# Top-32 attention and a gated feed-forward on one core: the sums of a softmax are spread before their reciprocal is taken

## The chip, the cores and the metric

The kernel runs on 1 core of a Trainium2 chip. The metric is the device time of one execution in microseconds (us); less is better. Before the change it is 1622.12 us, the median of 3 runs (1620.75 to 1624.53).

## The reference

```
scores = scale * q @ k.T                        # 8 batches, 8 heads, 576 positions, head size 64
kth    = the 32nd largest score of each row
scores = where(scores >= kth, scores, -1e9)
attn   = exp(scores - max(scores))
attn   = attn / (sum(attn) + 1e-9)
x      = (attn @ v), heads side by side         # 4608 tokens x 512
gate   = 1 / (1 + exp(-(x @ w_gate)))           # d_ff 1536
out    = (gate * (x @ w_val)) @ w_out           # all in float32
```

## The kernel before, in words

The attention goes tile by tile: a tile is 128 queries of two heads (a pair), or, where 576 leaves a rest of 64 queries, 64 of each head in one tile (then J is 1, else 2). For a tile TensorE makes the scores (`scores`, L203 and L219), ScalarE brings them to SBUF, VectorE searches the largest ones (`select`: MAX8 and MATCH_REPLACE8, L284 to L290), ScalarE and GpSimd mark and keep the scores under a bound (L296, L302, L303), VectorE finds the 32nd largest (L310), and ScalarE takes the exponentials e (L233). `masked` then zeroes in e what is under the 32nd largest and has VectorE accumulate the row's sum in the same instruction (L238). What follows in `masked` is the place of the change: GpSimd adds 1e-9 to the [128, J] sums (L241), VectorE takes their reciprocals (L242), and GpSimd spreads each of them over 128/J columns of a [128, 128] tile `inv` (L244).

`turn` turns e by TensorE transposes (L321, L326), ScalarE reads them out of PSUM (L322). `weigh` is called for one or two tiles of a pair: it multiplies the turned e with the values into one PSUM bank (`po`, L340 to L348), turns `inv` by a transpose into another part of the same bank (`rb`, L351), has ScalarE read the turned reciprocals into SBUF (`rs`, L354), and VectorE multiplies the output out of PSUM with them (`xf`, L357; for the rest of 64 queries L361). ScalarE and GpSimd split xf into two parts of lower precision, xh and xl (L364, L365). The pool of that bank has one buffer: the next `weigh` waits until xf has been read. There are 160 tiles and 112 calls of `weigh`, 48 with 256 columns of reciprocals and 64 with 128.

Three tiles of 128 tokens of all four pairs make a unit of 384 tokens. For it `ffn` runs the feed-forward part: matmuls with split operands (L396 to L398 into `pz`, L415 to L417 into `po`), Tanh, multiply and split on ScalarE, VectorE and GpSimd (L401 to L404), output by DMA. `run` lays attention and feed-forward work beside each other. In the first stage of the program, before any unit is ready, the weights are split as well (`split_weight`, L130 to L150: DMA, ScalarE, VectorE, GpSimd, TensorE, ScalarE, DMA), and the keys of later batches (L169, L171).

The order of instructions on each engine is drawn by the framework's scheduler from the dependences and its own costs; each engine then works strictly in that order. Names in the rows below end in numbers of tiles: xf_2_3 is tile 2 of pair 3.

Of the kernel before, what the change touches and what calls it, by code (L numbers as in the profile page):

```python
# [10 lines left out]
F32 = mybir.dt.float32  # L11
# [4 lines left out]
AF = mybir.ActivationFunctionType  # L16
ALU = mybir.AluOpType
# [11 lines left out]
def tile_topk_attention_then_gated_ffn(  # L29
# [8 lines left out]
    nc = tc.nc  # L38
    P = 128
    B, H, _, S = k.shape  # L40
# [194 lines left out]
    def masked(J, s, kth, st, e, nm):  # L235

        for j in range(J):
            nc.vector.scalar_tensor_tensor(  # L238
                e[:, j], s[:, j], kth[j], e[:, j], op0=ALU.is_ge, op1=ALU.mult, accum_out=st[:, 4 + j : 5 + j]
            )  # L240
        nc.gpsimd.tensor_scalar(st[:, 4 : 4 + J], st[:, 4 : 4 + J], 1e-9, None, op0=ALU.add)  # L241
        nc.vector.reciprocal(st[:, 6 : 6 + J], st[:, 4 : 4 + J])  # L242
        inv = bi.tile([P, P], F32, tag="inv", name=f"inv_{nm}")
        nc.gpsimd.tensor_copy(  # L244
            inv.rearrange("p (j d) -> p j d", j=J), st[:, 6 : 6 + J].unsqueeze(2).to_broadcast([P, J, P // J])
        )
        return e, inv

# [82 lines left out]

    def weigh(et, vt, n, invs, pieces, nm):

# [15 lines left out]

        for t, inv in enumerate(invs):  # L350
            nc.tensor.transpose(rb[:, t * P : (t + 1) * P], inv, ident)  # L351
        rs = b2.tile([P, 2 * P], F32, tag="rs", name=f"rs_{nm}")
        m = len(invs) * P
        nc.scalar.activation(rs[:, :m], rb[:, :m], AF.Copy)  # L354
        xf = b2.tile([P, 2 * P], F32, tag="xf", name=f"xf_{nm}")[:, :n]
# [72 lines left out]
    def run(general):  # L428
# [32 lines left out]
        for n in range(len(steps) + 2):  # L461
# [35 lines left out]
            nm = f"{mark}{b}_{i}_{p}"  # L497
            e, inv = done.pop(n - 2)
            if i == first or (i - first) % 2 == 0 or i == NT:
                et, o, invs = b2.tile([P, 9, 2 * P], F32, tag="et", name=f"et_{nm}"), 0, []  # L500
            turn(e, i, et, o, nm)
            invs.append(inv)
            o += P if i < NT else REM
            if len(invs) == 2 or i >= end - 1 or i == NT - 1:

                t, left, pieces = b * S + (i + 1 - len(invs)) * P, o, []
                while left:
# [10 lines left out]
                    t, left = t + k, left - k  # L518
                weigh(et, values[g, p], o, invs, pieces, nm)
            at += (P if i < NT else REM) / NP  # L520
# [76 lines left out]
```

## Time and profile before

| | |
|---|---|
| median of 3 runs | 1622.12 us (1620.75 to 1624.53) |
| the profiled execution | 1619.79 us |
| its span, first to last instruction | 1618.0 us |
| mean granted TensorE clock | 0.981 of 2.4 GHz |

The profile is of one execution, so a sum made from its rows is a sum against 1619.79 us; its span leaves out 1.8 us around the program. A busy time is the time in which an engine had at least one instruction at work. The idle time of an engine is put down to the instruction that it waited for last.

### The profile page before, as it was taken

The numbers are of one execution on the slowest core, as the hardware profiler recorded it, in microseconds if no ns is written. First come the engines' busy times: TensorE is split into PE (matmuls) and PEld (weight loads), VectorE is DVE, ScalarE is ACT, GpSimd is POOL, SyncE is SP. The second block draws the span as 40 slices with busy tenths as digits, with TensorE's granted clock in tenths as the row PEclk, the third lists the DMA queues.
The fourth block names the chain that finished last, engine by engine and source line by source line (L and its number), as shares of the span: only waits on it lengthen the run. The fifth ranks groups of instructions, "written<-read, shape, count | busy, mean of one in ns | idle before, by whom it ended". The sixth has DMA issues, their size and how long they took to land.

```text
span 1618.0 us, 33444 instructions
## 1 busy us (share of the span) xinstructions
PE 1553.3 (96%) x10226; PEld 1391.1 (86%) x10226; DVE 1265.3 (78%) x5748; ACT 1168.9 (72%) x2615; POOL 1206.8 (75%) x1923
## 2 busy tenths in 40 slices
PE   5878999899999999999999999999999999999998
PEld 2434897789999999999999999989999999999998
DVE  5999878988888779887888778888788778888300
ACT  6888778977777777777777777777777777777322
POOL 3679977897767896787877886788876996776413
PEclk9878999999999999999999999999999999999999
DMA  7556745665655565565555665655565665554575
GB/s 240 191 187 223 262 166 190 208 217 207 220 191 187 197 247 198 207 227 204 200 193 189 222 234 188 218 175 206 202 200 181 217 225 197 187 200 165 194 268 178
DMA packets 88989, 331.98 MB, mean 205 GB/s; under 512 B 9952, under 2 KB 36576, under 8 KB 61920
## 3 DMA queue, kind: packets, MB, share of 16 engines
q1 hardware_dynamic: 88800, 329.75, 59.0%
q8 instruction: 83, 1.36, 0.3%
q14 instruction: 106, 0.87, 0.2%
HBM read 301.40 MB, written 28.31 MB: 204 GB/s over the span
## 4 chain that ended last, share of the span: by engine, by line
PE 75%; POOL 7%; DVE 4%; ACT 3%; issue 1%; DMA 1%; POOLq 0%; SPq 0%; ACTq 0%
PE pz L396 11%; PE pz L397 11%; PE pz L398 11%; PE pss L219 8%; PE pt L321 6%; PE po L340 6%; PE po L415 5%; PE po L417 5%; PE po L416 5%; POOL u L302 3%; PE po L342 2%; DVE e L238 1%; PE po L351 1%; POOL k L171 1%; DVE kths L310 1%
## 5 line engine op out<-in xcount | busy, mean ns | idle before, releaser
L302 POOL TENSOR_TENSOR u<-s,under 128x288 f32<-128x288 f32 x576 | 444.5, 794 | 83.3 <-ACT under L296 77.3
L284 DVE MAX8 cand<-s 128x8 f32<-128x72 f32 x2304 | 348.1, 218 | 73.4 <-ACT s L226 63.3
L396 PE MATMUL pz<-xh,w 128*128 128x384 f32 x1120 | 383.9, 344 | 0.5 <-ACT gf L401 0.5
L397 PE MATMUL pz<-xl,w 128*128 128x384 f32 x1120 | 380.1, 339 | 0.3 <-POOL xl L365 0.3
L398 PE MATMUL pz<-xh,w 128*128 128x384 f32 x1120 | 379.5, 339 | 0.0
L238 DVE SCALAR_TENSOR_TENSOR e<-s,kths,e 128x576 f32<-128x576 f32 x288 | 291.7, 1020 | 2.8 <-ACT e L233 2.7
L310 DVE MAX8 kths<-u 128x8 f32<-128x584 f32 x288 | 219.6, 763 | 88.5 <-POOL u L303 86.3
L296 ACT ACTIVATE under<-s,leads 128x576 bf16<-128x576 f32 x288 | 223.4, 777 | 43.1 <-DVE leads L288 38.1
L233 ACT ACTIVATE e<-s,st 128x576 f32<-128x576 f32 x288 | 210.1, 774 | 52.0 <-POOL st L292 51.3
L404 POOL TENSOR_TENSOR gl<-gf,gh 128x384 fp32r<-128x384 f32 x144 | 156.0, 1084 | 92.4 <-ACT gh L403 90.3
L322 ACT ACTIVATE et<-pt 128x384 f32<-128x384 f32 x384 | 179.8, 490 | 46.4 <-PE pt L321 45.8
L396 PEld LDWEIGHTS pz<-xh,w 128*128 128x128 f32 x1120 | 210.8, 188 | 1.7 <-ACT gf L401 1.0
L397 PEld LDWEIGHTS pz<-xl,w 128*128 128x128 f32 x1120 | 211.4, 189 | 1.0 <-POOL xl L365 0.6
L398 PEld LDWEIGHTS pz<-xh,w 128*128 128x128 f32 x1120 | 211.1, 189 | 0.0
L226 ACT ACTIVATE s<-pss 128x576 f32<-128x576 f32 x256 | 164.5, 643 | 42.1 <-PE pss L219 41.4
L416 PE MATMUL po<-gl,w 128*128 128x384 f32 x560 | 189.5, 340 | 0.4 <-POOL gl L404 0.3
L415 PE MATMUL po<-gh,w 128*128 128x384 f32 x560 | 188.8, 350 | 0.9 <-ACT acc L419 0.9
L321 PE MATMUL pt<-ident,e 128*128 128x128 f32 x1152 | 184.9, 279 | 4.9 <-DVE e L238 2.6
L417 PE MATMUL po<-gh,w 128*128 128x384 f32 x560 | 187.4, 338 | 0.0
L321 PEld LDWEIGHTS pt<-ident,e 128*128 128x128 f32 x1152 | 144.7, 143 | 28.9 <-DVE e L238 6.5
L219 PE MATMUL pss<-k,qh 128*128 128x288 f32 (+2 forms) x588 | 167.5, 303 | 2.0 <-ACT s L226 2.0
L219 PE MATMUL pss<-k,ql 128*128 128x288 f32 (+2 forms) x588 | 159.1, 293 | 0.0
(105 smaller groups left out, 3318.6 us busy)
## 6 DMA issues: line engine op xcount, KB each, us to landing
w<-ws SPq DMA_DIRECT2D x210, 1024.0 KB, 4.9
v<-in_v_dram SPq DMA_DIRECT2D x64, 352.0 KB, 3.3
wraw<-in_w_dram SPq DMA_DIRECT2D x36, 512.0 KB, 4.4
ws<-wsplit SPq DMA_DIRECT2D x36, 512.0 KB, 3.5
qraw<-in_q_dram SPq DMA_DIRECT2D x140, 128.0 KB, 3.0
kraw<-in_k_dram SPq DMA_DIRECT2D x56, 288.0 KB, 3.8
out_dram<-acc SPq DMA_DIRECT2D x48, 192.0 KB, 4.0
q<-in_q_dram SPq DMA_DIRECT2D x20, 128.0 KB, 3.5
```

The lines of the kernel that those rows point to most:

```text
L219: nc.tensor.matmul(ps[:, half, o : o + n], x[:K, h * P : (h + 1) * P], ks[h][:K, k0 : k0 + n], start=t == 0, stop=t == len(todo) - 1,)
L238: nc.vector.scalar_tensor_tensor(e[:, j], s[:, j], kth[j], e[:, j], op0=ALU.is_ge, op1=ALU.mult, accum_out=st[:, 4 + j : 5 + j])
L284: nc.vector.max(cand[:, j, 8 * g : 8 * g + 8], s[:, j, g * SEG : (g + 1) * SEG])
L302: nc.gpsimd.tensor_tensor(u[:, j, c], s[:, j, c], under[:, j, c], op=ALU.mult)
L310: nc.vector.max(kths[:, at[j] : at[j] + 8], u[:, j])
L321: nc.tensor.transpose(pt[:, c], ef[:, k0 : k0 + P], ident)
L396: nc.tensor.matmul(ps, wt[:, u, 0, d], xh, start=d == 0, stop=False)
L397: nc.tensor.matmul(ps, wt[:, u, 0, d], xl, start=False, stop=False)
L398: nc.tensor.matmul(ps, wt[:, u, 1, d], xh, start=False, stop=d == NP - 1)
L415: nc.tensor.matmul(ps, wt[:, e % 2, 0, f], gh, start=f == 0, stop=False)
L416: nc.tensor.matmul(ps, wt[:, e % 2, 0, f], gl, start=False, stop=False)
L417: nc.tensor.matmul(ps, wt[:, e % 2, 1, f], gh, start=False, stop=f == FG - 1)
```

## The change

In `masked` the sums go to GpSimd alone: one instruction reads the [128, J] sums as a broadcast, adds 1e-9 and writes the [128, 128] tile, now `wide`. The small reciprocal goes. `weigh` turns `wide` as it turned `inv`, and in place of ScalarE's copy VectorE takes the reciprocal of the turned sums while it reads them out of PSUM. The rest of the diff renames `inv` and `invs`.

```
-        nc.gpsimd.tensor_scalar(st[:, 4 : 4 + J], st[:, 4 : 4 + J], 1e-9, None, op0=ALU.add)
-        nc.vector.reciprocal(st[:, 6 : 6 + J], st[:, 4 : 4 + J])
-        inv = bi.tile([P, P], F32, tag="inv", name=f"inv_{nm}")
-        nc.gpsimd.tensor_copy(
-            inv.rearrange("p (j d) -> p j d", j=J), st[:, 6 : 6 + J].unsqueeze(2).to_broadcast([P, J, P // J])
-        )
-        return e, inv
+        wide = bi.tile([P, P], F32, tag="wide", name=f"wide_{nm}")
+        nc.gpsimd.tensor_scalar(
+            wide.rearrange("p (j d) -> p j d", j=J),
+            st[:, 4 : 4 + J].unsqueeze(2).to_broadcast([P, J, P // J]),
+            1e-9,
+            None,
+            op0=ALU.add,
+        )
+        return e, wide
...
-        for t, inv in enumerate(invs):
-            nc.tensor.transpose(rb[:, t * P : (t + 1) * P], inv, ident)
+        for t, wide in enumerate(wides):
+            nc.tensor.transpose(rb[:, t * P : (t + 1) * P], wide, ident)
         rs = b2.tile([P, 2 * P], F32, tag="rs", name=f"rs_{nm}")
-        m = len(invs) * P
-        nc.scalar.activation(rs[:, :m], rb[:, :m], AF.Copy)
+        m = len(wides) * P
+        nc.vector.reciprocal(rs[:, :m], rb[:, :m])
```

VectorE's order around the last multiply of the first unit, xf_2_3. Before (L242 is the small reciprocal, cand, tops and leads belong to the search, kths and e to L310 and L238, wraw and wt_lead to the split of a weight):

```order
L310 MAX kths<-u_4_0_1756 128x8
L290 MATCH_REPLACE cand_3_1_1831<-tops_3_1_1832,cand_3_1_1831 128x64
L288 MAX leads<-cand_3_1_1831 128x8
L284 MAX cand_4_1_1925<-s_4_1_1743 128x8 x8
L238 SCALAR_TENSOR_TENSOR e_4_0_1755,st_4_0_1753<-s_4_0_1567,kths,e_4_0_1755 128x576
L288 MAX leads<-cand_3_1_1831 128x8
L242 RECIPROCAL st_3_0_1657<-st_3_0_1657 128x2
L138 TENSOR_SCALAR wt_lead_0_2967<-wt_lead_0_2967 128x512
L288 MAX tops_4_1_1926<-cand_4_1_1925 128x8
L357 TENSOR_TENSOR xf_2_3_1814<-po_2_3_1801,rs_2_3_1812 128x128
L242 RECIPROCAL st_4_0_1753<-st_4_0_1753 128x1
```
Now (lines after the change in `masked` stand 2 higher, L356 is the reciprocal out of PSUM, L359 the multiply):

```order
L292 MATCH_REPLACE cand_3_1_1805<-tops_3_1_1806,cand_3_1_1805 128x64 x2
L286 MAX cand_4_1_1897<-s_4_1_1719 128x8 x8
L140 TENSOR_SCALAR wt_lead_1_1530<-wraw_1_1528 128x512
L290 MAX tops_3_1_1806<-cand_3_1_1805 128x8 x2
L356 RECIPROCAL rs_2_3_1786<-po_2_3_1775 128x128
L290 MAX tops_4_1_1898<-cand_4_1_1897 128x8
L292 MATCH_REPLACE cand_3_1_1805<-tops_3_1_1806,cand_3_1_1805 128x64 x2
L138 TENSOR_SCALAR wt_lead_0_2925<-wt_lead_0_2925 128x512
L359 TENSOR_TENSOR xf_2_3_1788<-po_2_3_1775,rs_2_3_1786 128x128
L292 MATCH_REPLACE cand_4_1_1897<-tops_4_1_1898,cand_4_1_1897 128x64
L290 MAX leads<-cand_3_1_1805 128x8
```
The multiply stands at nearly the same place. Its reciprocal rs_2_3 stands four rows in front of it, with searches and a step of a weight split between them, and the small reciprocals are gone from both sides.

TensorE's order where the feed-forward part begins (`pz` with xh and xl). Before (wrest belongs to the split of a weight, pss are scores, pt turned exponentials):

```order
L219 MATMUL pss_4_1_0_1744<-k_1_3_321,q_4_1_1565 128x64
L147 MATMUL wrest_0_1534<-wsplit_1530,minus 128x512
L148 MATMUL wrest_0_1534<-wsplit_1530,plus 128x512
L146 MATMUL wrest_1_1551<-wraw_1_1548,ident 128x512
L396 MATMUL pz_0_0_0_1963<-xh_0_614,w_0_1959 128x384
L397 MATMUL pz_0_0_0_1963<-xl_0_615,w_0_1959 128x384
L398 MATMUL pz_0_0_0_1963<-xh_0_614,w_0_1959 128x384
L396 MATMUL pz_0_0_0_1963<-xh_1_996,w_0_1959 128x384
L397 MATMUL pz_0_0_0_1963<-xl_1_997,w_0_1959 128x384
L398 MATMUL pz_0_0_0_1963<-xh_1_996,w_0_1959 128x384
L396 MATMUL pz_0_0_0_1963<-xh_2_1378,w_0_1959 128x384
L397 MATMUL pz_0_0_0_1963<-xl_2_1379,w_0_1959 128x384
```
Now (L342 to L344 are the weighing, L353 the transpose of `wide`, L398 to L400 the feed-forward):

```order
L342 MATMUL po_2_3_1775<-et_2_3_1759,v_3_1044 64x128
L343 MATMUL po_2_3_1775<-et_2_3_1759,v_3_1044 64x128
L344 MATMUL po_2_3_1775<-et_2_3_1759,v_3_1044 128x128
L353 MATMUL po_2_3_1775<-ident,wide_2_3_1680 128x128
L323 MATMUL pt_3_0_2_1863<-ident,e_3_0_1637 128x128 x3
L146 MATMUL wrest_1_1531<-wraw_1_1528,ident 128x512
L398 MATMUL pz_0_0_0_1933<-xh_0_608,w_0_1929 128x384
L399 MATMUL pz_0_0_0_1933<-xl_0_609,w_0_1929 128x384
L400 MATMUL pz_0_0_0_1933<-xh_0_608,w_0_1929 128x384
L398 MATMUL pz_0_0_0_1933<-xh_1_984,w_0_1929 128x384
L399 MATMUL pz_0_0_0_1933<-xl_1_985,w_0_1929 128x384
```
The first feed-forward matmuls stood behind the split's wrest_1 and in front of the turns of tile 3_0 and of the weighing po_2_3. Now they stand behind all turns of tile 3_0 and behind the weighing po_2_3 with its transpose.

## Rows read from the trace of the kernel before

**Rows 1.** The page's first part: busy time of each engine, its share of the span, and its instructions (PEld is TensorE's weight load, DVE VectorE, ACT ScalarE, POOL GpSimd).

```profile
PE 1553.3 (96%) x10226; PEld 1391.1 (86%) x10226; DVE 1265.3 (78%) x5748; ACT 1168.9 (72%) x2615; POOL 1206.8 (75%) x1923
```

**Rows 2.** Busy time by stage of the span. Columns: the stage in us and its length, then for each engine its busy us with the number of its instructions, then the granted TensorE clock as a share of 2.4 GHz, the busy share of the DMA engines, and GB/s.

```profile
0.00:160.00 160.00, 117.27 (x467) 60.07 (x467) 136.75 (x596) 127.88 (x258) 106.74 (x177) 0.84 0.64 210
160.00:360.00 200.00, 190.29 (x1231) 164.14 (x1230) 173.01 (x743) 159.65 (x356) 170.22 (x263) 0.99 0.61 212
360.00:1500.00 1140.00, 1134.49 (x7855) 1059.14 (x7854) 938.78 (x4373) 850.75 (x1935) 892.27 (x1442) 1.00 0.59 202
1500.00:1618.00 118.00, 111.21 (x680) 107.74 (x678) 16.79 (x40) 30.57 (x67) 37.54 (x43) 0.99 0.60 213
```

**Rows 3.** The waits of TensorE's matmuls from 360 to 1500 us, longest first: who waited for whom, us in total, times, longest.

```profile
PE pt L321 <- ACT et L322: 2.2, 1, 2.2
PE pss L219 <- ACT s L226: 1.8, 1, 1.8
```

**Rows 4.** TensorE's timeline where the feed-forward part begins: the first matmul of it and the ninth, with seven more between them. Columns: start, us, engine, line, operation, output and inputs, shapes.

```profile
161.23 0.76 PE L396 MATMUL pz<-xh,w 128*128 128x384 f32 x1
...
163.05 0.34 PE L398 MATMUL pz<-xh,w 128*128 128x384 f32 x1
```

**Rows 5.** Busy time by stretch, with the columns of rows 2: the first stage after the start-up, its last 40 us, and two stretches in which the splitting of weights goes on.

```profile
40.00:160.00 120.00, 96.11 (x408) 50.99 (x406) 113.85 (x480) 103.47 (x213) 92.24 (x140) 0.82 0.59 200
120.00:160.00 40.00, 33.54 (x143) 19.22 (x139) 39.34 (x169) 35.55 (x75) 36.05 (x53) 0.83 0.67 223
240.00:280.00 40.00, 37.71 (x221) 30.26 (x218) 36.60 (x152) 34.44 (x78) 32.09 (x47) 0.96 0.52 173
280.00:320.00 40.00, 35.72 (x208) 28.34 (x206) 38.34 (x143) 37.07 (x79) 34.90 (x48) 1.00 0.65 226
```

**Rows 6.** The chain of work that ended last up to 165 us, followed back in time: start, us, engine, tile and line.

```profile
143.30 1.37 POOL wsplit L143 x2
144.67 0.69 POOL inv L244
...
145.76 3.79 POOL k L171 x4
...
149.61 2.00 POOL wsplit L143 x2
...
151.66 0.70 PE wrest L148
```

**Rows 7.** Groups of instructions over the whole span, each shape apart: line, engine, operation, output and inputs with their shapes, number | busy us, mean ns of one | idle time of the engine just before them, and who ended it.

```profile
L241 POOL TENSOR_SCALAR st<-st 128x2 f32<-128x2 f32 x128 | 30.9, 242 | 38.9 <-DVE e L238 29.9 <-ACT qh L188 0.9
L241 POOL TENSOR_SCALAR st<-st 128x1 f32<-128x1 f32 x32 | 7.2, 225 | 7.4 <-DVE e L238 5.1
L242 DVE RECIPROCAL st<-st 128x2 f32<-128x2 f32 x128 | 19.7, 154 | 15.3 <-POOL st L241 14.6
L242 DVE RECIPROCAL st<-st 128x1 f32<-128x1 f32 x32 | 5.0, 156 | 12.2 <-POOL st L241 12.2
L244 POOL COPY inv<-st 128x128 f32<-128x128 f32 x160 | 54.1, 339 | 40.0 <-DVE st L242 35.8 <-PE po L351 0.8 <-DVE tops L288 0.4
L354 ACT ACTIVATE rs<-po 128x256 f32<-128x256 f32 x48 | 18.2, 379 | 20.2 <-PE po L351 20.1
L354 ACT ACTIVATE rs<-po 128x128 f32<-128x128 f32 x64 | 17.3, 270 | 15.7 <-PE po L351 15.3
L357 DVE TENSOR_TENSOR xf<-po,rs 128x256 f32<-128x256 f32 x48 | 19.7, 410 | 11.1 <-ACT rs L354 9.1 <-POOL xl L365 2.0
L357 DVE TENSOR_TENSOR xf<-po,rs 128x128 f32<-128x128 f32 x32 | 8.8, 276 | 1.6 <-ACT rs L354 1.5
L361 DVE TENSOR_TENSOR xf<-po,rs 64x64 f32<-64x64 f32 x64 | 13.7, 215 | 8.9 <-ACT rs L354 8.5
L365 POOL TENSOR_TENSOR xl<-xf,xh 128x128 fp32r<-128x128 f32 x32 | 17.1, 535 | 3.5 <-ACT xh L364 2.3
L536 DVE TENSOR_SCALAR bad<-bad 128x1 f32<-128x1 f32 x1 | 0.2, 154 | 0.0
L351 PE MATMUL po<-ident,inv 128*128 128x128 f32 x160 | 37.8, 284 | 0.0
```

**Rows 8.** Waits by pair: who waited for whom, us in total, times, longest. The first two rows are of the stretch from 160 to 360 us, the third of 360 to 1500 us.

```profile
ACT rs L354 <- PE po L351: 8.4, 5, 2.3
DVE st L242 <- POOL st L241: 5.5, 7, 1.6
DVE st L242 <- POOL st L241: 20.6, 30, 1.5
```

**Rows 9.** The same stages for single lines: the stage and its length, busy us of that line's instructions with their number, then the clock and the DMA columns. The first three rows are VectorE's small reciprocal (L242), the next three ScalarE's read of the turned sums (L354).

```profile
0.00:160.00 160.00, 1.77 (x12) 0.84 0.64 210
160.00:360.00 200.00, 3.28 (x22) 0.99 0.61 212
360.00:1500.00 1140.00, 19.34 (x125) 1.00 0.59 202
0.00:160.00 160.00, 2.34 (x7) 0.84 0.64 210
160.00:360.00 200.00, 4.76 (x15) 0.99 0.61 212
360.00:1500.00 1140.00, 27.07 (x86) 1.00 0.59 202
```

More of the change, by code (lines that the diff above doesn't have):

```diff
@@ L330, in turn, with weigh @@
             nc.scalar.activation(et[:REM, 4, :P], pt[:REM, 0], AF.Copy)
-    def weigh(et, vt, n, invs, pieces, nm):
+    def weigh(et, vt, n, wides, pieces, nm):
         both = ps_o.tile([P, 4 * P], F32, tag="o", name=f"po_{nm}")
@@ L497, in run @@
             nm = f"{mark}{b}_{i}_{p}"
-            e, inv = done.pop(n - 2)
+            e, wide = done.pop(n - 2)
             if i == first or (i - first) % 2 == 0 or i == NT:
-                et, o, invs = b2.tile([P, 9, 2 * P], F32, tag="et", name=f"et_{nm}"), 0, []
+                et, o, wides = b2.tile([P, 9, 2 * P], F32, tag="et", name=f"et_{nm}"), 0, []
             turn(e, i, et, o, nm)
-            invs.append(inv)
+            wides.append(wide)
             o += P if i < NT else REM
-            if len(invs) == 2 or i >= end - 1 or i == NT - 1:
-                t, left, pieces = b * S + (i + 1 - len(invs)) * P, o, []
+            if len(wides) == 2 or i >= end - 1 or i == NT - 1:
+                t, left, pieces = b * S + (i + 1 - len(wides)) * P, o, []
                 while left:
@@ L518, in run @@
                     t, left = t + k, left - k
-                weigh(et, values[g, p], o, invs, pieces, nm)
+                weigh(et, values[g, p], o, wides, pieces, nm)
             at += (P if i < NT else REM) / NP
```

## The prediction

> **What bounds the kernel now.** I read the page's busy line first: TensorE (PE) is at work in 1553.3 us of a span of 1618.0, VectorE in 1265.3, GpSimd in 1206.8, ScalarE in 1168.9 [rows 1]. A share of the whole span does not say where a change pays, so I cut the span into stages [rows 2]. From 360 to 1500 us PE is busy 1134.5 of 1140 us: what the other engines do there is paid for only where it makes PE wait, and of the 5.5 us that PE lacks the two longest waits of its matmuls, behind ScalarE, are 4.0 [rows 3]. Nothing there waits for the multiply of the output or for the turned sums. The room is in front of it: PE is idle 160 − 117.3 = 42.7 us in the first 160 us, 200 − 190.3 = 9.7 us in the next 200. In the first stage no feed-forward matmul exists yet, because the first unit of attention output isn't done; the first one starts at 161.23 us [rows 4]. There the pace is VectorE's: after a start-up of 40 us it is busy 113.9 of 120 us [rows 5], and the granted clock is 0.82, between its levels of 1.2 and 2.4 GHz, since PE works and waits by turns. The chain that ends the stage passes through GpSimd as well [rows 6]: the split of a weight (L143), the copy that spreads the sums (L244) and the key splits (L171) stand in one queue in front of PE's L148. After 1500 us attention is over and PE works off matmuls alone; nothing of the change is in its way. So a gain or loss of the whole program has to be made in the first 360 us, or by a new wait of PE behind it.
>
> **What the change removes and adds.** Per tile 160 times, GpSimd's add on [128, 2] sums (L241) and VectorE's reciprocal (L242) go, and the copy L244 becomes an add of the same output. Per group of tiles 112 times, ScalarE's read of the turned sums (L354) goes, and VectorE reads them with a reciprocal. PE's instructions stay the same ones: 160 transposes (L351). No DMA is added or removed.
>
> *GpSimd.* It loses 30.9 + 7.2 us of L241 and 54.1 of L244 [rows 7]. The new instruction has L244's output and its broadcast input and adds a constant: no less than the copy, 339 ns, and no more than a two-input instruction of 128 columns, 535 ns (L365). It is nearest to the copy; I take 360 ns, 57.6 us for 160. Sum −34.6 us, at the upper end −6.6.
>
> *ScalarE.* −18.2 − 17.3 = −35.5 us [rows 7], nothing added.
>
> *VectorE.* It loses 19.7 + 5.0 = 24.7 us of small reciprocals, and 26.8 us in which it stood waiting for L241: 20.6 of them from 360 to 1500 us and 5.5 from 160 to 360, the rest once at the very end [rows 8]. It gains 48 reciprocals of 256 columns and 64 of 128, out of PSUM. No row shows a wide reciprocal. The nearest rows are the multiplies out of the same bank, L357, 410 and 276 ns, which is 134 ns per 128 columns. [...] So 48 × 0.410 + 64 × 0.276 = 37.4 us, net +12.7 busy and −26.8 of waiting.
>
> **By stage.** *0 to 160 us:* twelve small reciprocals go, 1.8 us [rows 9], and no waiting. ScalarE's 7 reads took 2.34 us, which at 379 and 270 ns are 4 of 256 and 3 of 128: 4 × 0.410 + 3 × 0.276 = 2.5 us. Net +0.7, and VectorE sets the pace for 114 of 120 us: +0.6. *160 to 360 us:* −3.3 and −5.5 of waiting, and for 15 reads of 4.76 us 6.5 × 0.410 + 8.5 × 0.276 = +5.0: −3.8 us of VectorE's time. PE is idle only 9.7 us there, and its waits are for several engines, so I let a quarter through: −1.0. *360 to 1500 us:* VectorE gets 19.3 + 20.6 us back and pays 35 × 0.410 + 51 × 0.276 = 28.4; PE is full, 0. *After:* 0.
>
> *The order.* The scheduler draws the order anew. Up to the multiply that ends the first unit (xf_2_3) VectorE has nearly the same work. But PE's first feed-forward matmuls now stand behind the last weighing of the unit and behind the turns of tile 3_0. In the kernel before, the first nine started between 161.23 and 163.05 us [rows 4], with the last one's step a filler of 2.0 us. If PE has nothing else, that filler is missing; if the instructions now ahead are ready, nothing is. Bounds 0 and +2.0; I take +0.4, since PE's first stretch is otherwise paced by VectorE.
>
> *The shorter road to the sums.* Accumulator, GpSimd, VectorE, GpSimd, PE becomes accumulator, GpSimd, PE. That is worth nothing by itself: PE's matmul L351 never once stood idle for its input (its row has no idle time [rows 7]). If this cover went, the next in line would be the single PSUM bank that holds output and turned sums.
>
> Sum: +0.6 − 1.0 + 0 + 0.4 = 0.0 us on the profiled execution's 1619.79. The median of the three runs, 1622.12, lies 2.3 above that execution, so the changed kernel should come out at 1622.0. A measurement tells 0.2% from nothing here, 3.2 us; I forecast no change.
>
> **Rivals.** *Relief in front (faster).* If GpSimd is what PE waits for in the first 360 us, as [rows 6] has it just before 152 us, its relief counts: 34 of the 160 tiles fall in these stages [rows 9], so 34/160 of 34.6, 7.4 us, beside 7.1 of ScalarE. For it: GpSimd stands at 36.1 of 40 us from 120 to 160 [rows 5]. Against it: VectorE is fuller in every one of these rows. Half of GpSimd's relief gives 1618.4, all of it 1614.7; I take 1616. With VectorE's own 3.8 us on top it is 1611.
>
> *The wait changes engines (slower).* ScalarE stood 8.4 us in five pieces before L354 from 160 to 360 us because PE hadn't turned the sums [rows 8]. Now VectorE stands there, with the searches (MAX8) for the next tiles' candidates queued behind it; GpSimd and ScalarE wait for those, and PE for them. If all 8.4 us fall on VectorE and reach PE, less the 3.8 it saved: +4.6, some 1627; without that saving 1630.5. It decides from about 7 us of VectorE's idle time before the new reciprocal in the first 360 us. Against it: the multiply behind L354 needed the same turned sums, and VectorE waited for it only 19 us in all [rows 7]; the order leaves other instructions between.
>
> [...]
>
> [...]
>
> **How the numbers follow.** My forecast has 0.46, relief in front 0.24, the moved wait 0.18, the slow reciprocal 0.12. The first lies within 0.2%, the second is faster, the last two slower: faster 0.24, same 0.46, slower 0.30. The forecast's own range is 1619 to 1625. The whole range goes from 1612, the relief with most of VectorE's saving on top, to 1633, the moved wait at its dearest with the order's 2.0 us; out of it are the slow reciprocal and the tips of the others, under 2 in 10.
>
> **What would show it.** Right: reciprocals near 410 and 276 ns; the new GpSimd instruction at 340 to 400; PE's first feed-forward matmul within 3 us of 161, PE idle 50 to 53 us in the first 360, full from 360 to 1500; VectorE busy some 13 us more. Wrong: reciprocals over 1 us; over 7 us of VectorE's idle time before them ahead of 360 us; PE's idle time in the first 360 us under 47 us; or new waits of PE in the middle.

## The result, and the profile after

The changed kernel takes 1633.17 us (median of 4 runs, 1632.91 to 1635.14) against 1623.21 us of the kernel before in the same comparison: ratio 1.0062 [1.0048, 1.0076], some 10 us slower. No change was forecast. Its profiled execution has a span of 1631.1 us.

The page's first part for the changed kernel, against [rows 1]:

```profile
PE 1551.2 (95%) x10226; PEld 1386.2 (85%) x10226; DVE 1345.9 (83%) x5700; ACT 1141.6 (70%) x2503; POOL 1213.3 (74%) x1763
```

VectorE has 80.6 us more, where the forecast had 12.7. ScalarE has 27.3 less. GpSimd, which was to lose 34.6, has 6.5 more. The groups of instructions that the change made, with the columns of [rows 7], say why:

```profile
L242 POOL TENSOR_SCALAR wide<-st 128x128 f32<-128x128 f32 x160 | 90.8, 567 | 70.5 <-DVE e L238 55.5 <-DVE tops L290 4.2 <-PE pz L400 1.0
...
L356 DVE RECIPROCAL rs<-po 128x256 f32<-128x256 f32 x48 | 83.7, 1744 | 9.7 <-PE po L353 9.5
...
L356 DVE RECIPROCAL rs<-po 128x128 f32<-128x128 f32 x64 | 60.7, 949 | 22.0 <-PE po L353 21.9
L353 PE MATMUL po<-ident,wide 128*128 128x128 f32 x160 | 37.9, 285 | 0.0
...
L359 DVE TENSOR_TENSOR xf<-po,rs 128x256 f32<-128x256 f32 x48 | 19.7, 410 | 0.0
```

The wide reciprocal takes 1744 and 949 ns, the multiply of the same columns still 410. GpSimd's fused instruction takes 567 ns, so that 160 of them (90.8 us) cost what the add and the copy cost before (30.9 + 7.2 + 54.1 = 92.2). The stages of the changed kernel, with the columns of [rows 2]:

```profile
0.00:160.00 160.00, 109.85 (x449) 54.77 (x449) 136.89 (x565) 122.79 (x243) 102.36 (x158) 0.86 0.62 197
160.00:360.00 200.00, 184.24 (x1162) 153.27 (x1163) 178.58 (x728) 154.36 (x336) 166.17 (x236) 0.97 0.60 202
360.00:1500.00 1140.00, 1132.71 (x7851) 1058.46 (x7850) 1000.98 (x4338) 826.73 (x1842) 901.29 (x1319) 1.00 0.59 204
1500.00:1632.00 132.00, 124.42 (x768) 119.69 (x766) 29.42 (x72) 37.76 (x83) 43.50 (x53) 0.98 0.56 205
```

Since PE's matmuls are the same ones, the span is read as PE's busy time plus its idle time. Busy: 1551.2, 2.1 less than before. Idle: 160 − 109.9 = 50.2 us in the first stage (before 42.7), 15.8 in the second (9.7), 7.3 in the third (5.5). Of the growth of 15.2 us, 13.5 lie in the first 360 us. From 360 us on VectorE carries 62 us more, and PE loses 1.8. At 1500 us PE has 768 matmuls left where it had 680.

VectorE's and PE's timelines where the first unit ends (start, us, engine, line, operation; in brackets the idle time before and who ended it), to be held against 161.23 us in [rows 4]:

```profile
173.95 0.96 DVE L356 RECIPROCAL rs<-po 128x128 f32<-128x128 f32 x1 [0.19 <-PE po L353]
...
175.91 0.28 DVE L359 TENSOR_TENSOR xf<-po,rs 128x128 f32<-128x128 f32 x1
```

```profile
174.56 0.76 PE L398 MATMUL pz<-xh,w 128*128 128x384 f32 x1
```

The first feed-forward matmul is 13.3 us late. Whether that carries the loss is a question for the experiments.

### The profile page after: what moved, and what is told of

It reads as the page before. It is cut to its first block, busy times and chain, and to the rows that moved or that the text cites. A ratio compares the mean times of both kernels' runs of the same rounds, so it can differ in the third digit from the quotient of the medians.

```text
span 1631.1 us, 33252 instructions
## 1 busy us (share of the span) xinstructions
PE 1551.2 (95%) x10226; PEld 1386.2 (85%) x10226; DVE 1345.9 (83%) x5700; ACT 1141.6 (70%) x2503; POOL 1213.3 (74%) x1763
## 4 chain that ended last, share of the span: by engine, by line
PE 71%; DVE 8%; POOL 6%; ACT 3%; issue 2%; DMA 2%; POOLq 0%; ACTq 0%
PE pz L398 10%; PE pz L399 10%; PE pz L400 10%; PE pss L219 8%; PE pt L323 5%; PE po L342 5%; PE po L417 5%; PE po L418 5%; PE po L419 5%; POOL u L304 2%; PE po L344 2%; DVE e L238 2%; DVE cand L286 2%; DVE kths L312 2%; DMA wraw<-in_w_dram 2%
## 5 line engine op out<-in xcount | busy, mean ns | idle before, releaser
L304 POOL TENSOR_TENSOR u<-s,under 128x288 f32<-128x288 f32 x576 | 449.4, 804 | 67.1 <-ACT under L298 57.8
L398 PE MATMUL pz<-xh,w 128*128 128x384 f32 x1120 | 384.0, 344 | 0.3 <-ACT gf L403 0.3
L400 PE MATMUL pz<-xh,w 128*128 128x384 f32 x1120 | 378.9, 338 | 0.0
L238 DVE SCALAR_TENSOR_TENSOR e<-s,kths,e 128x576 f32<-128x576 f32 x288 | 285.5, 994 | 1.9 <-ACT e L233 1.7
L298 ACT ACTIVATE under<-s,leads 128x576 bf16<-128x576 f32 x288 | 223.0, 776 | 48.8 <-DVE leads L290 42.2
L398 PEld LDWEIGHTS pz<-xh,w 128*128 128x128 f32 x1120 | 210.6, 188 | 2.0 <-issue 0.6
L400 PEld LDWEIGHTS pz<-xh,w 128*128 128x128 f32 x1120 | 211.0, 188 | 0.0
L219 PE MATMUL pss<-k,qh 128*128 128x288 f32 (+2 forms) x588 | 167.5, 303 | 6.2 <-ACT s L226 6.2
L356 DVE RECIPROCAL rs<-po 128x256 f32<-128x256 f32 (+1 forms) x112 | 144.4, 1290 | 31.7 <-PE po L353 31.3
```

Source lines behind the costliest of these rows:

```text
L219: nc.tensor.matmul(ps[:, half, o : o + n], x[:K, h * P : (h + 1) * P], ks[h][:K, k0 : k0 + n], start=t == 0, stop=t == len(todo) - 1,)
L238: nc.vector.scalar_tensor_tensor(e[:, j], s[:, j], kth[j], e[:, j], op0=ALU.is_ge, op1=ALU.mult, accum_out=st[:, 4 + j : 5 + j])
L304: nc.gpsimd.tensor_tensor(u[:, j, c], s[:, j, c], under[:, j, c], op=ALU.mult)
L398: nc.tensor.matmul(ps, wt[:, u, 0, d], xh, start=d == 0, stop=False)
L400: nc.tensor.matmul(ps, wt[:, u, 1, d], xh, start=False, stop=d == NP - 1)
```

## The experiments

The table sums up the profiles of all versions. "Idle" is the idle time of PE up to 160 us, from 160 to 360, and after; the ratio is to the kernel before on the same chip. A profile is of one execution, which need not lie at the median: e12's took 1628.42 us, 2.6 over its median.

| version | median us | ratio [95%] | PE busy | PE idle by stage |
|---|---|---|---|---|
| before | 1623.2 | 1 | 1553.3 | 42.7, 9.7, 12.3 |
| changed | 1633.17 | 1.0062 [1.0048, 1.0076] | 1551.2 | 50.2, 15.8, 14.0 |
| e1 plain read | 1619.45 | 0.9987 [0.9976, 0.9997] | 1546.5 | 48.4, 15.0, 9.7 |
| e2b ScalarE reads | 1622.74 | 0.9994 [0.9985, 1.0003] | 1551.1 | 46.1, 14.5, 11.9 |
| e3 all but the first tiles | 1627.21 | 1.0022 [1.0012, 1.0033] | 1549.7 | 47.7, 14.9, 14.2 |
| e4 first tiles only | 1632.80 | 1.0069 [1.0056, 1.0083] | 1556.3 | 50.1, 11.2, 14.1 |
| e5 idle reciprocals | 1628.43 | 1.0032 [1.0021, 1.0044] | 1552.5 | 48.0, 15.9, 12.0 |
| e6 chunks upwards | 1639.70 | 1.0101 [1.0086, 1.0116] | 1569.4 | 46.0, 13.2, 11.0 |
| e7 VectorE adds | 1627.17 | 1.0026 [1.0016, 1.0035] | 1550.5 | 47.6, 12.8, 14.4 |
| e8 widths | 1623.69 | one run | 1553.3 | 46.1, 10.6, 11.9 |
| e12 two steps | 1625.86 | 1.0024 [1.0015, 1.0033] | 1553.2 | 46.1, 13.6, 13.6 |
| e17 two steps, plain read | 1624.50 | 1.0007 [0.9998, 1.0017] | 1551.9 | 48.8, 12.3, 9.8 |
| e9 swap: before | 1661.53 | 1.0246 [1.0232, 1.0260] | 1592.6 | 45.6, 14.3, 9.9 |
| e10 swap: changed | 1674.62 | 1.0326 [1.0312, 1.0340] | 1595.0 | 48.7, 17.5, 13.0 |
| e11 swap: plain read | 1650.70 | 1.0175 [1.0161, 1.0189] | 1584.6 | 48.0, 12.2, 6.9 |
| e16 swap: two steps | 1662.81 | 1.0235 [1.0215, 1.0255] | 1585.8 | 47.2, 15.5, 14.5 |
| e13 turn first: before | 1629.67 | 1.0036 [1.0024, 1.0048] | 1551.1 | 45.0, 17.6, 12.3 |
| e14 turn first: changed | 1632.08 | 1.0056 [1.0035, 1.0076] | 1552.4 | 47.2, 12.5, 17.6 |
| e15 turn first: two steps | 1626.10 | 1.0014 [1.0001, 1.0027] | 1552.2 | 49.3, 13.2, 11.7 |
| e18 no add | 1610.18 | 0.9924 [0.9912, 0.9937] | 1545.5 | 47.0, 7.6, 8.1 |

Up to 1500 us e8 runs the instructions of the kernel before in the same order (what it adds starts at 1533 us), so its row shows how far two executions of one program differ: PE's busy time not at all, its idle time by 3.8 us, 3.4 of them in the first stage. Differences in idle time of some 4 us are therefore not shown by one profile each. Against e8 the changed kernel has +11.4 us of idle time and −2.1 of busy time, which is the 9.3 us between their spans and nearly the 10 us between the medians; 9.2 of the idle time lie in the first 360 us.

### Is it the duration of the read?

e1: the fused instruction stays, VectorE reads without dividing.

```
-        nc.vector.reciprocal(rs[:, :m], rb[:, :m])
+        nc.vector.tensor_copy(rs[:, :m], rb[:, :m])
```

> The changed kernel with one line different: VectorE reads the turned sums out of PSUM with a plain copy in place of the reciprocal (the division is left out). Theory 'slow': the 112 reciprocals cost 1744 and 949 ns where a plain read costs about 410 and 276, and 8 of them stand in front of the first unit (4 x 1.33 + 3 or 4 x 0.67 = some 8 us), so the time comes back to 1621 to 1627 us and PE's first feed-forward matmul starts at 160 to 167 us instead of 174.6. Theory 'moved wait' (VectorE stands for PE's turned sums wherever the read is on VectorE): stays at 1630 to 1635. Theory 'GpSimd' (the fused instruction at 567 ns holds PE's transposes up): stays at 1630 to 1635.

e2b: the same with ScalarE reading, as before the change.

```
-        nc.vector.reciprocal(rs[:, :m], rb[:, :m])
+        nc.scalar.activation(rs[:, :m], rb[:, :m], AF.Copy)
```

> The changed kernel with ScalarE's copy back in place of VectorE's reciprocal; no reciprocal is left in it (the division is left out). So only the fused GpSimd instruction of the change remains, and VectorE has 13 small reciprocals fewer in front of the first unit than before the change. 'Slow' and 'moved wait': 1618 to 1624 us, since neither the wide reciprocal nor a wait of VectorE for PE is there. 'GpSimd': 1630 or more.

e3 and e4 divide the change by tiles: `masked` and `weigh` get a switch. It is on in e4 for the first 12 tiles only, which hold 8 of the 112 wide reciprocals, and in e3 for all others.

```
+    def turned(g):
+        return g < 1          # e4; in e3 g >= 1
```

> The change is made only for tiles after the first 12 (the first unit of the four pairs keeps the old way). If the loss is made in front of PE's first feed-forward matmul, as 'slow' says: 1621 to 1627 us, although 104 of the 112 wide reciprocals remain. If it is made by the reciprocals wherever they stand (VectorE too full from 160 us on, or PE's new waits in the middle): 1628 to 1633.

> The mirror: the change is made only for the first 12 tiles (8 wide reciprocals), everything after is the old way. 'Slow in front of the first unit': 1629 to 1634 us, with PE's first feed-forward matmul at 170 to 176 us. Loss spread over all reciprocals: under 1625.

The read of e1, with the columns of [rows 7]:

```profile
L356 DVE COPY rs<-po 128x256 f32<-128x256 f32 x48 | 19.9, 414 | 8.2 <-PE po L353 8.0
...
L356 DVE COPY rs<-po 128x128 f32<-128x128 f32 x64 | 18.0, 281 | 17.9 <-PE po L353 17.5
```

414 and 281 ns: the same read, out of the same bank, without the division. The kernel is then not slower than before, and with ScalarE's read it is equal to it. The change in the first 12 tiles alone (8 reciprocals, 10.7 us of VectorE, with their fused instructions) gives as much as the whole change; the other 104 reciprocals of e3 (134 us) come with 3.6 us. So the change hurts most in the first tiles, and the division has a hand in it. But the loss doesn't add up over the tiles (10 + 4 against 10), and by stage the case is weaker than by time. Of the 11.5 us between the profiled executions of e1 and the changed kernel, 2.5 are PE's idle time up to 360 us, 4.3 its idle time after, and 4.7 its busy time. Up to 360 us e1 is still idle 6.7 us longer than e8, and in e4 3.1 of the 9.9 us over e8 are busy time.

e2b and e4 lie in the ranges of 'slow', e3 between its two ranges, and e1 under its own. One expectation of e1 fell: its first feed-forward matmul started at 173.78 us, as late as in the changed kernel (174.56), and yet the time came back. A late first unit doesn't make the kernel slower by itself; whether it has a part in e1's 6.7 us of idle time is not shown.

e5 puts 8 reciprocals whose result nobody reads into the kernel before, one in `masked` for each of tiles 1 and 2 of the first batch's four pairs:

```
+        if more:                              # 256 columns for tile 1, 128 for tile 2 of the first batch
+            idle = b2.tile([P, 2 * P], F32, tag="xf", name=f"idle_{nm}")
+            nc.vector.reciprocal(idle[:, :more], s[:, 0, :more])
```

> The kernel before with 8 extra wide reciprocals in front of the first unit (256 columns for the middle tile of each pair, 128 for the last), taken of the scores in SBUF right behind the mask, their results never used. Nothing of the change is in it. Theory 'occupancy' (what counts is VectorE's time before the first unit is done): 8 x about 1.35 us = 10.8 us more of VectorE there, so 1630 to 1636 us. Theory 'latency' (what counts is that the wide reciprocal stands between the turned sums and the multiply): under 1626, as the path from the sums to the output is the old one.

They took 1734 and 937 ns, and the kernel took 5.3 us more, between the two expectations. It may be that occupying VectorE for 10.6 us in that stage costs about half of it. But e5 has another drawn order as well, and a redrawn order alone cost 6 us in e13 (below), so this is not shown.

e8 measures the price by width: after the last unit single instructions run out of SBUF (psrc) and PSUM (ptwo).

```
+    for r in range(3):
+        for n in (1, 2, 8, 32, 64, 128, 256):
+            nc.vector.reciprocal(dst[:, 0, :n], src[:, :n])
+            nc.vector.reciprocal(dst[:, 1, :n], two[:, :n])
...
+        nc.gpsimd.tensor_scalar(pool_dst[:, 0, :P].rearrange("p (j d) -> p j d", j=2), spread, 1e-9, None, op0=ALU.add)
+        nc.gpsimd.tensor_scalar(pool_dst[:, 1, :P], src[:, :P], 1e-9, None, op0=ALU.add)
```

> The kernel before with a row of single instructions behind its last output: reciprocals of 1, 2, 8, 32, 64, 128 and 256 columns out of SBUF and out of PSUM, plain copies out of PSUM, and GpSimd's add and copy of 128 columns from a broadcast and from a plain input. 'Cost per column': a straight line of about 6.2 ns per column above a fixed part (949 and 1744 ns), so 1 and 2 columns would differ by 6 ns and 8 columns would be 40 ns above 2; 'fixed start of a wide instruction': no line through the small ones. The data are all 3.0: if the duration hangs on the data, 128 and 256 columns come out other than 949 and 1744. GpSimd: the add from a broadcast at 529 to 567 ns when alone, if its cost is the instruction's own; near the copy's 290 if it was contention.

```profile
L541 DVE RECIPROCAL pdst<-ptwo 128x256 f32<-128x256 f32 x3 | 5.1, 1716 | 0.0
...
L541 DVE RECIPROCAL pdst<-ptwo 128x128 f32<-128x128 f32 x3 | 2.8, 934 | 0.0
...
L541 DVE RECIPROCAL pdst<-ptwo 128x64 f32<-128x64 f32 x3 | 1.6, 534 | 0.0
L547 POOL TENSOR_SCALAR pooldst<-psrc 128x128 f32<-128x128 f32 x3 | 1.6, 534 | 0.2
L546 POOL TENSOR_SCALAR pooldst<-psrc 128x128 f32<-128x128 f32 x3 | 1.6, 533 | 3.3 <-PE po L417 3.1
...
L541 DVE RECIPROCAL pdst<-ptwo 128x8 f32<-128x8 f32 x3 | 0.6, 207 | 0.0
...
L540 DVE RECIPROCAL pdst<-psrc 128x2 f32<-128x2 f32 x3 | 0.5, 156 | 0.0
```

From 128 to 256 columns a reciprocal grows by (1716 − 934) / 128 = 6.1 ns per column, from PSUM as from SBUF; at 2 columns nothing of that is to be seen. So 'cost per column' held, and with all data 3.0 the price is the kernel's to 2%. GpSimd's add of a constant to 128 columns takes 534 ns whether its input is spread or not, so the spreading isn't what makes it dear.

### Is it the order that was drawn?

e6 writes the chunks of the weighing upwards, e9 swaps its two matmuls; neither contains any part of the change.

```
-            for c in reversed(range(4)):      # e6; start=c == 3 becomes start=c == 0
+            for c in range(4):
...
-                nc.tensor.matmul(po[D:], vt[:, 6 + c], et[:, 5 + c, :n], start=c == 3, stop=False)
                 nc.tensor.matmul(po[:D], vt[:, c], et[:, c, :n], start=c == 3, stop=False)
+                nc.tensor.matmul(po[D:], vt[:, 6 + c], et[:, 5 + c, :n], start=c == 3, stop=False)   # e9
```

> The kernel before with the four matmul pairs of the weighing written in rising instead of falling order. No instruction is added, removed or resized; the scheduler draws another order on all engines (PE's first feed-forward matmul moves from place 319 to 361). Theory 'order' (a good part of the loss is the order drawn anew): off by 3 us or more from the kernel before, to either side. 'Slow reciprocal' alone: within 3 us of the kernel before, 1620 to 1626.

> The kernel before with the two matmuls of a column chunk in the weighing written in the other order: the same instructions, no part of the change, but the scheduler draws another order (TensorE's first feed-forward matmul at place 370, in the kernel before 319). Theory 'slow reads' (the loss is the occupancy of VectorE by reciprocals of 1.74 and 0.95 us in front of the first unit): no such reads here, so 1618 to 1627 us, TensorE idle under 60 us in the first 360. Theory 'order' (the redrawn order decides, as it does by 16 us where the column chunks run upwards): it may come out anywhere, and over 1629 us would show that a redrawn order alone is worth as much as the change.

+16.6 and +39.9 us without any other instruction. But this is another thing than the change's loss. PE's busy time with matmuls that write a `po` (of the weighing and of the feed-forward part), summed over the whole span, first the kernel before, then e6, then e9:

```profile
sum 1700.00, PE 575.10; mean PE 287.55
```

```profile
sum 1700.00, PE 590.04; mean PE 295.02
```

```profile
sum 1700.00, PE 610.89; mean PE 305.45
```

Here PE's *busy* time grew, by 14.9 and 35.8 us. The weighing's own matmuls, those that read `et`, were busy 212.2 us before, 222.6 in e6 and 245.3 in e9. The timelines show two things. The matmuls of L340 and L341 stood in 90 unbroken stretches before and stand in 146 and 147 now: the scheduler puts other work into the middle of a weighing. And in e9 some 290 of their 1280 records start without a partner to the other half of `po`, where in the kernel before and in e6 it is 12. A weighing of e6, torn apart, with its halves still together (L219 are scores):

```profile
410.93 0.38 PE L340 MATMUL po<-et,v 128*64 128x256 f32 x1
410.93 0.38 PE L341 MATMUL po<-et,v 128*64 128x256 f32 x1
...
412.44 0.29 PE L219 MATMUL pss<-k,qh 128*128 128x288 f32 x1
...
413.06 0.43 PE L340 MATMUL po<-et,v 128*64 128x256 f32 x1
413.06 0.43 PE L341 MATMUL po<-et,v 128*64 128x256 f32 x1
```

PE's idle time in e6 and e9 (70.2 and 69.8 us) is that of e8 (68.5). So the expectation of e9 failed in time and held in idle time. Nor does e6 show that the order makes the change's loss: e6 lost busy time, the change idle time.

The swap was kept as a second base, in which the change and the plain read were made again:

> The changed kernel with the same swap of two matmuls in the weighing: the change whole, in another drawn order (first feed-forward matmul at place 342, changed kernel 340). Theory 'slow reads': 1629 to 1638 us, TensorE idle over 62 us in the first 360, whatever the order. Theory 'order': the loss belongs to the one order that was drawn, so a new draw is as likely to give 1618 to 1626 us.

> The swapped changed kernel with VectorE reading the turned sums by a plain copy (the division by the sums is left out), first feed-forward matmul at place 334. Theory 'slow reads': reads of 410 and 280 ns and 1616 to 1626 us, at least 7 us under the swapped changed kernel. Theory 'order': no fixed relation to the swapped changed kernel, the difference may lie on either side of zero.

The levels were missed with the base. The differences have the sign that the slow reads ask for: the change costs 13.1 us here, the plain read takes away 23.9. Of these 23.9, 10.4 are PE's busy time, 6.1 its idle time up to 360 us and 6.0 after (profiled executions, 22.5 apart).

### Is it GpSimd's fused instruction?

e12 leaves GpSimd its two steps and moves only the reciprocal; e17 is the same with the plain read; e7 is the kernel before with the add on VectorE.

```
+        nc.gpsimd.tensor_scalar(st[:, 4 : 4 + J], st[:, 4 : 4 + J], 1e-9, None, op0=ALU.add)
+        nc.gpsimd.tensor_copy(
+            wide.rearrange("p (j d) -> p j d", j=J), st[:, 4 : 4 + J].unsqueeze(2).to_broadcast([P, J, P // J])
+        )
```

> Only the second half of the change: GpSimd adds 1e-9 to the sums and spreads them with a copy, in two instructions as before, and VectorE takes the reciprocal out of PSUM. Theory 'slow reads': 1629 to 1637 us, the same as the changed kernel, and the fused instruction of GpSimd is worth under 3 us either way. Rival 'GpSimd' (the fused instruction of 567 ns, slower than the copy it takes the place of, holds up the splits behind it): under 1628 us.

> The missing corner: GpSimd adds and copies in two steps, VectorE reads the turned sums by a plain copy (the division by the sums is left out). If the fused instruction costs 6 to 7 us by itself, whatever the read: 1611 to 1614 us, as much under the fused one with a plain read (1619.5) as two steps with slow reads are under the changed kernel. If the fused instruction costs only beside slow reads, or the difference is the draw of the order: 1617 to 1626 us. If slow reads cost 10 us by themselves: at least 8 us under two steps with slow reads (1625.9), so under 1618.

```
-        nc.gpsimd.tensor_scalar(st[:, 4 : 4 + J], st[:, 4 : 4 + J], 1e-9, None, op0=ALU.add)
+        nc.vector.tensor_scalar(st[:, 4 : 4 + J], st[:, 4 : 4 + J], 1e-9, None, op0=ALU.add)
```

> The kernel before with the add of 1e-9 on VectorE in front of its small reciprocal, in place of GpSimd's: one GpSimd instruction and one change of engine per tile fewer, no wide reciprocal, ScalarE's read kept. A candidate to beat both kernels. VectorE gets 160 instructions of about 0.15 us, 12 of them (some 1 to 2 us) before the first unit, and loses the 26.8 us of waiting for GpSimd, most of it after 360 us where it costs nothing. If occupancy before the first unit decides: 1621 to 1626; if the waits for GpSimd cost PE anything: under 1620.

With the same slow reciprocals, two steps cost 1.0024 where the fused instruction costs 1.0062: the rival named in e12 is the one that held. e17 fell where the fused instruction costs only beside slow reads, or the order decides. e7 missed both of its ranges: at 1.0026 it is slower than the kernel before, so the add didn't pay on VectorE either.

e17 closes the square. In idle time of PE (one profile each, so to some 4 us): plain read 70.9 with two steps and 73.1 fused; reciprocal 73.4 and 79.9. The division adds 2.5 beside two steps and 6.8 beside the fused instruction, the fusion 2.2 and 6.5. The 2.5 and 2.2 lie within the scatter of two executions, and e12's 73.4 is from an execution over its median. None of these versions has less idle time than the kernel before (64.7, in e8 68.5). In medians the square is more uneven (1624.5, 1619.5, 1625.9, 1633.2), since PE's busy time in e1 is 6.7 us under before.

A road from the two to PE was looked for in the waits of the first 160 us: GpSimd waiting for VectorE, and PE waiting for GpSimd's split of a weight (us, times, longest). The kernel before, where GpSimd waited at two places for a tile's sums:

```profile
POOL st L241 <- DVE e L238: 4.9, 4, 2.7
POOL inv L244 <- DVE st L242: 4.7, 3, 2.1
...
PE wrest L148 <- POOL wsplit L143: 3.4, 5, 1.2
```

The changed kernel, GpSimd's wait, then PE's:

```profile
POOL wide L242 <- DVE e L238: 11.3, 5, 4.6
...
PE wrest L148 <- POOL wsplit L143: 9.9, 6, 3.1
```

Two steps with the reciprocal (e12):

```profile
POOL st L242 <- DVE e L238: 7.4, 4, 4.6
...
PE wrest L148 <- POOL wsplit L143: 6.8, 5, 2.9
```

Fused with the plain read (e1):

```profile
POOL wide L242 <- DVE e L238: 4.0, 4, 1.8
...
PE wrest L148 <- POOL wsplit L143: 4.7, 3, 2.2
```

Two steps with the plain read (e17):

```profile
POOL st L242 <- DVE e L238: 3.9, 4, 1.8
...
PE wrest L148 <- POOL wsplit L143: 3.5, 3, 2.2
```

The longest such wait of the changed kernel on VectorE's timeline, and on GpSimd's:

```profile
70.60 0.96 DVE L356 RECIPROCAL rs<-po 128x128 f32<-128x128 f32 x1 [0.70 <-PE po L353]
...
72.24 0.80 DVE L238 SCALAR_TENSOR_TENSOR e<-s,kths,e 128x576 f32<-128x576 f32 x1
```

```profile
73.21 1.01 POOL L242 TENSOR_SCALAR wide<-st 128x128 f32<-128x128 f32 x1 [4.60 <-DVE e L238]
75.70 1.29 POOL L367 TENSOR_TENSOR xl<-xf,xh 128x128 fp32r<-128x128 f32 x1 [1.48 <-ACT xh L366]
...
77.38 2.30 POOL L143 TENSOR_TENSOR wsplit<-wsplit,wt_lead 128x256 fp32r<-128x256 f32 x3
```

The reciprocal stands in front of e on VectorE, e is late, GpSimd stands 4.60 us at its fused instruction (1.83 in e1, 2.69 at L241 before), and the splits that PE needs stand behind it. In this base the two waits rise together from the plain reads to the changed kernel.

That is a road, but it doesn't carry the loss. GpSimd stands as long in e12 (4.63 us at its add), which loses little. And PE waits at two more places for the split of a weight, for VectorE (L146) and for ScalarE (L147). Before:

```profile
PE wrest L146 <- DVE wraw L139: 16.7, 7, 5.5
...
PE wrest L147 <- ACT wsplit L145: 6.9, 6, 1.8
```

In the changed kernel:

```profile
PE wrest L146 <- DVE wraw L139: 14.9, 7, 5.0
...
PE wrest L147 <- ACT wsplit L145: 3.3, 3, 2.2
```

All three together are 27.0 us before, 30.3 in e8 and 28.1 in the changed kernel: what PE waits longer for GpSimd, it waits less for the other two. Over the first 360 us, PE's waits for other engines are 9.3 us longer in the changed kernel than in e8 (58.8 against 49.5). By what PE was to do, that is 4.7 more before scores, 4.4 before turns and 3.1 before feed-forward matmuls into `pz`, and 3.0 less before the split. Which instruction starts this was not traced.

Whether the fused instruction is a loss everywhere was tried in the swapped base (e16) and in a third one, where the turns of the sums are written ahead of the weighing:

```
         po, rb = both[:, :n], both[:, 2 * P :]
+        for t, inv in enumerate(invs):
+            nc.tensor.transpose(rb[:, t * P : (t + 1) * P], inv, ident)
```

> Two steps on GpSimd with the reciprocal out of PSUM, in the base with the two matmuls of a column chunk swapped, where the kernel before took 1661.5 us and the changed one 1674.6. If the fused GpSimd instruction costs some 6 us by itself: 1666 to 1670 us. If the slow reads carry the loss and the rest is the draw of the order: 1668 to 1682 us, above or below the changed one.

> The kernel before with the turns of the spread sums written ahead of the matmuls of the weighing: the same instructions, another drawn order, a third base beside the kernel before and the swapped one. Theory 'slow reads': no slow read, TensorE's idle time in the first 360 us under 60 us; its own time is a draw of the order, 1618 to 1632 us. Theory 'order': the same, with no bound on the idle time.

> The changed kernel in the base with the turns ahead of the weighing. Theory 'slow reads': 5 to 14 us over the kernel before in this base, as it is 10 in the first base and 13 in the swapped one. Theory 'order': within 5 us of it, on either side. Turning first also lets VectorE take the reciprocal while TensorE still weighs; if the wait for the slow reciprocal (and not VectorE's occupancy) is what costs, the difference falls under 4 us.

> Two steps on GpSimd (add, then copy) with the reciprocal out of PSUM, in the base with the turns ahead of the weighing. If the fused GpSimd instruction costs some 6 us by itself, this is 4 to 8 us under the changed kernel of this base. If the 7 us between the two in the first base were the draw of the order, it may be on either side, within 8 us.

Two steps are quicker than the fused instruction in all three bases: by 0.38, 0.91 and 0.42% in the ratios, 7.3, 11.8 and 6.0 us in the medians. In the swapped base the time lies under both ranges of e16, and 9.2 us of the gain are PE's busy time. Nor is the gain made in one place: up to 360 us, two steps save 6.2 and 3.6 us of idle time in the first two bases, and in the third they have 2.8 more and save it after 360 us. Two steps with slow reciprocals against the kernel before of each base: +0.24, −0.11 and −0.22%; the first is a loss clear of noise, and over the three bases there is none.

The change itself costs 0.62, 0.80 and 0.20%. In the third base its cost is 2.4 us in the medians of e13 and e14, taken on one chip; only one of the ten runs of e13 lies above any of the six of e14. That is under the 5 to 14 us of 'slow reads', so this expectation failed there; the difference is that of the theory 'order', and also the one foreseen if the wait for the reciprocal is what costs. The run cannot tell these two apart. In this base the kernel before was itself idle 17.6 us from 160 to 360 us, so its expectation of under 60 us was missed (62.6), and up to 360 us the changed kernel is idle 2.9 us less than it. GpSimd's wait for e is not a rule either: in e10 it was only 1.4 us in the first 160.

### A version that beats both

> A version meant to beat both: the kernel before without GpSimd's add of 1e-9. Each sum holds the term of the row's maximum, exp(0) = 1, so that adding 1e-9 in float32 gives the same number and nothing is left out. GpSimd loses 160 instructions and 38 us, the chain to the turned sums one step, nothing is added. If GpSimd's time in the first 360 us reaches TensorE: 1614 to 1619 us. If it doesn't (theory of the prediction): 1619 to 1626 us. A worse draw of the order: over 1627.

1610.18 us (5 runs, 1609.75 to 1612.51), ratio 0.9924 [0.9912, 0.9937], and GpSimd's add is gone from its rows. Its stages, with the columns of [rows 2]:

```profile
0.00:160.00 160.00, 113.00 (x465) 55.54 (x466) 134.24 (x579) 128.85 (x260) 103.92 (x164) 0.86 0.67 210
160.00:360.00 200.00, 192.44 (x1219) 164.09 (x1219) 170.88 (x749) 156.44 (x351) 166.14 (x241) 0.97 0.62 210
360.00:1500.00 1140.00, 1139.17 (x7945) 1067.43 (x7944) 946.30 (x4405) 853.97 (x1949) 868.77 (x1330) 1.00 0.59 204
```

PE is idle 62.6 us, 5.9 under e8, and busy 1545.5, 7.8 less, with the same 10226 matmuls. So the larger part of the gain is PE's busy time, which no run ties to the missing add. The smaller part is idle time: 3.0 us less from 160 to 360 us and 3.8 after, 0.9 more before. The time lies under all three ranges of the expectation. It was not tried in a second base, so e18 is a quicker kernel, but it is not shown that the add made it so.

## Why the prediction was wrong, point by point

**What bounds the kernel** held for the change: 9.2 of its 11.4 us of idle time over e8 came up in the first 360 us, and the middle hid 62 us of added VectorE work at 1.8 us of PE's idle time. It is no rule for the other versions: e1 and e11 got back 4.3 and 6.0 us of idle time after 360 us, against the changed kernel of their base, and several gained or lost PE's busy time, for which the prediction had no term.

**VectorE's term is the step that failed.** The wide reciprocal was taken at the multiply's 410 and 276 ns. No run shows it at that price; it takes 1744 and 949. The small reciprocals of the rows, 154 and 156 ns at 2 and 1 columns, could not decide: e8 shows 156 ns at 2 columns and 1716 at 256 in the same instruction. The slope of the wide ones doesn't show at 1 and 2 columns at all (156 ns each out of SBUF). The prediction said that no row shows a wide reciprocal and gave the multiply's price most of the chance all the same. The 0.12 of the slow reciprocal is the author's estimate; no row shows a price for it, and the runs showed 1744 and 949 ns, in the changed kernel (949 − 276) / 128 = 5.3 ns per column over the multiply. With the prices of the rows the reciprocals come to 48 × 1.744 + 64 × 0.949 = 144.4 us in place of 37.4.

**GpSimd's term failed too.** The fused instruction was put at 360 ns with 535 as its upper end, because it looked most like the copy. It took 567 in the kernel and 533 alone. The 34.6 us of relief became 1.4. In three bases the fusion is a loss beside slow reciprocals, though not each time in the same stage.

**By stage**, in idle time: +0.6 came out as +7.5 (of which 3.4 lie within the scatter of two executions), −1.0 as +6.1, 0 as +1.8, 0 after 1500 us as −0.1; PE's busy time −2.1. So 1622 was 11 us too low, for the most part in its first two stages, and 62 us of VectorE's time in the middle cost next to nothing (1.8 us). The slow reciprocal alone doesn't make up the first two: beside two steps (e12) it cost 4 us, so they belong to the reciprocal and the fused instruction together. That 1633.17 lies next to the upper end of the whole range, 1633, is luck: that end was made of the moved wait, which was not what happened.

**The order** was given +0.4 with bounds 0 to 2.0. Too narrow: e13, a redrawn order with the same PE busy time to 2.1 us, is 0.36% off, some 6 us, and e1 and e18 have 7 to 8 us less of PE's busy time with the same matmuls. The nine matmuls on which the term was built were 13 us late, and in e1 as late without a loss of time. The term was sized by nine matmuls, and an order is drawn for all of them.

**The moved wait** didn't decide. VectorE's wait before the reciprocal in the first 360 us:

```profile
DVE rs L356 <- PE po L353: 3.3, 5, 1.2
```

3.3 us, under the 7 at which it was to count. **Relief in front** was not tested by the change, since there was no relief. e18 made it; its idle time up to 160 us is not lower than e8's. **The shorter road** was worth nothing, as forecast: the turn L353 has no idle time, as L351 had none.

**Left open**: by what road the slow reciprocal and the fused instruction reach PE, and why the fused instruction hurts beside the reciprocal and hardly beside a plain read. The prices of both are shown, and so is that mending either one takes most of the loss away in the first base. But the queue in front of the splits doesn't carry the loss, and the order can't be taken out of the account: each edit draws a new one, a new one alone is worth 6 us (e13), and no version had the changed kernel's exact order and a quick read.

## What to carry to other kernels

An instruction seen only at one or two columns has no price at 128 (here 156 ns at 2 and 934 at 128, e8): measure two widths before choosing one. Removing a hop is not a gain in itself: here the merged instruction cost what the two had cost (90.8 us against 92.2). A wait that grows is no proof of a loss: add up all waits for the same work before naming a road, since one engine's wait can take the place of another's. Where a scheduler draws the order anew, read a small difference as PE's busy and idle time apart, by stage, and try an edit in a second base before believing it.

## What the runs showed of the hardware

From 128 to 256 columns VectorE's reciprocal costs 6.1 ns per column, 6.2 out of SBUF (e8); the rest, some 120 to 150 ns, is an estimate of its fixed part from these two widths. A plain read costs 1.0 to 1.3 per column (e1, e8). GpSimd adds a constant to 128 columns in 534 ns, spread input or not, and copies them in 292 to 297 (e8). In the kernel before, two matmuls to the two halves of `po` start within 0.01 us of each other and run side by side (at 400.92 and 400.93 us, 0.43 us each). In e9, where many start without a partner and weighings are torn apart, the same matmuls of the weighing were busy 245.3 us in place of 212.2; e6, torn apart only, 222.6. The granted TensorE clock of the kernel before is at 1.00 or at 0.50 of 2.4 GHz: 1.00 from 85 to 90 us, 0.50 from 91 to 100, 1.00 from 101 to 110. It drops to 0.50 ten times, and in the 3.4 us ahead of each drop PE is idle for 1.3 us or more.
